# One output-projection burst per head pair, later batch-0 masks and unread matmuls in a fused attention and gated MLP kernel

## Chip, cores, metric

The kernel runs on one core of a Trainium2 chip. The metric is device microseconds of the whole program. The profile adds one execution with every instruction; its span is about 2 us below the program's time.

## The reference, cut to what matters

```python
# attention: B=8 batches, H=8 heads, S=576 queries, 16 extra "beacon" keys, D=64
k_all = concat([beacon_k, k]); v_all = concat([beacon_v, v])
scores = q @ k_all.T / sqrt(64)          # causal over the 576 keys, beacons always visible
a = softmax(scores)
x = (a @ v_all), heads side by side      # 4608 tokens x 512
# gated MLP, d_ff = 1536
out = (gelu(x @ w_gate) * (x @ w_val)) @ w_out
```

Inputs and output are float32; the kernel computes matmuls in bfloat16.

## The kernel before

One batch is 576 tokens: eight heads as four *pairs*, two heads side by side on the 128 partitions. Per pair the kernel computes transposed scores in four chunks (a, b, c, d), exponentials on ScalarE, a causal mask on the diagonal blocks, the attention product together with a product with ones (which gives the softmax denominator), and the division. The gate and value matmuls of a 512-token chunk follow after each batch, and the output projection of the chunk before (48 matmuls of 512 columns) is spread through the next batch's attention, so that TensorE has something to do while ScalarE computes exponentials. A run of such output matmuls without a break is called an *output burst* here. Batches 1 to 7 repeat the same order of work and are called *steady*; their *distance* is the time from the first output burst of one to that of the next. All engines keep program order.

```python
psum_s: 2 buffers of 2 banks   # scores, gate/value products, "wide" attention products
psum_x: 1 buffer               # attention product x_ps (x and denominator), some transposes
psum_o: 1 buffer               # output projection

def scores(b, m, c):           # chunk c of pair m: matmuls, exponential, mask
    s_ps = psum_s.tile(...)
    for t, s_lo, w, col in CHUNKS[c]:
        for hi in range(2):    # two heads on two 64-row halves of the array
            mm(s_ps[:, hi, col:col+w], qkT[r, m, 1, ...], qkT[r, m, 0, ...], True, True)
    act(expT[:, :, o:o+w], s_ps[:, :, 0:w], ACT.Exp, scale=QK_SCALE)
    # ... then for each diagonal block of the chunk:
    #   b == 0: nc.vector.tensor_tensor(min with tri);  b > 0: nc.gpsimd.affine_select

def normalize(b, m, by_act=False):
    x_sb, rec_sb = npool.tile(...), npool.tile(...)
    if by_act:                 # 1/z = exp(-ln z) on ScalarE
        act(ln_sb, z_ps, ACT.Ln)
        nc.vector.tensor_copy(x_sb, x_ps)
        act(rec_sb, ln_sb, ACT.Exp, scale=-1.0)
    else:                      # VectorE: transpose, reciprocal of one column per block, transpose back
        if m == NPAIR - 1: nc.vector.transpose(zT_sb, z_ps)      # "z first" for the last pair
        act(x_sb, x_ps, ACT.Copy)
        if m < NPAIR - 1:  nc.vector.transpose(zT_sb, z_ps)
        nc.vector.reciprocal(r_sb, ...); nc.vector.transpose(rec_sb, ...)
    nc.vector.tensor_tensor(out=xT_sb[:, m, ...], in0=x_sb, in1=rec_sb, op=ALU.mult)

# ab(m) = scores chunks a, b; cd(m) = chunks c, d; av(m) = attention product and normalize;
# o(n) = the next n output-projection matmuls of the chunk before
if b == 0:
    ab(0); transpose_pe(0,1); cd(0); ab(1); transpose_pe(0,2); cd(1); ab(2); transpose_pe(0,3)
    cd(2); ab(3); av(0); cd(3); av(1, by_act=True); av(2, wide=True); av(3, by_act=True)
else:
    o(6); ab(0); o(8); cd(0); o(6); ab(1); o(4); av(0); cd(1); o(3); ab(2); av(1)
    o(3); cd(2); o(4); ab(3); o(2); av(2); cd(3); o(5); av(3); o(7)
# then 12 x gate_val (8 matmuls, Gelu, multiply); the first leaves the two that need pair 3 to its end
# [cut: loads, DMA transposes of q and k from batch 2 on, the last stage]
```

The softmax here doesn't subtract the row's maximum and nothing guards it: scores larger than these inputs give would overflow.

Of the kernel before, what the change touches and what calls it, by code (L numbers as in the profile page):

```python
# [7 lines left out]
P = 128  # L8
B, H, S, NB, D = 8, 8, 576, 16, 64
SK = S + NB  # L10
N_TOK = B * S
D_MODEL = 512
# [40 lines left out]
def kernel(  # L53
# [59 lines left out]
    def load_qk6(b, h0, h1):  # L113
        if b not in qk6:
            qk6[b] = (
                hpool.tile([P, 2, H, 6 * D], BF16, name="qk6", tag="hT_sb"),
                npool.tile([NB, H, D], BF16, name="kb", tag="kb"),
            )
        for w, src in enumerate((q, k)):
            dma(  # L120
                qk6[b][0][0:96, w, h0:h1, :],
                src[b, h0:h1, :, :].rearrange("h (p r) d -> p h (r d)", r=6),
            )
# [30 lines left out]
    def mm(out_ap, lhsT, rhs, start, stop, **kw):  # L154
        keep(nc.tensor.matmul(out_ap, lhsT, rhs, start=start, stop=stop, **kw))  # L155

    def act(out_ap, in_ap, func, **kw):
        keep(nc.scalar.activation(out_ap, in_ap, func, **kw))  # L158


    def transpose_pe(b, m, pool, tag):
        t_ps = pool.tile([P, 3 if tag == "x" else 2, 1024], BF16, name="t_ps", tag=tag)
        qk, kb = qk6[b]

        def tr(out_ap, in_ap):
            n = in_ap.shape[0]
            keep(nc.tensor.transpose(out_ap, in_ap, ident[0:n, 0:n]))  # L167

        for w in range(2):
            for r in range(6):  # L170
                for hi in range(2):
                    tr(
                        t_ps[64 * hi : 64 * hi + 64, w, r * 96 : (r + 1) * 96],
                        qk[0:96, w, 2 * m + hi, r * D : (r + 1) * D],
                    )
        tr(t_ps[:, 1, S:SK], kb[:, 2 * m : 2 * m + 2, :])
        keep(
            nc.vector.tensor_copy(  # L178
                qkT[:, m, :, NB:SK].rearrange("p w (t r) -> p w t r", r=6),
                t_ps[:, 0:2, 0:S].rearrange("p w (r t) -> p w t r", r=6),  # L180
            )
        )
        keep(nc.vector.tensor_copy(qkT[:, m, 1, 0:NB], t_ps[:, 1, S:SK]))  # L183

    def transpose_dma(b):
        q_sb, k_sb = q_ring[b % NRING], k_ring[b % NRING]
        for j in range(5):
            for w, src, n, c in ((0, q_sb, P if j < 4 else 64, NB), (1, k_sb, P if j < 4 else 80, 0)):
                keep(
                    nc.sync.dma_start_transpose(  # L190
                        out=qkT[:, :, w, c + j * P : c + j * P + n],
                        in_=src[0:n, j, :, :].rearrange("p h d -> p (h d)"),
                    )
                )
# [3 lines left out]
    def scores(b, m, c):  # L198
        i = b * NPAIR + m
        if c == 0:  # L200
            exp_of[i] = epool.tile([P, 2, EXP_W], BF16, name="expT", tag="expT")
        expT = exp_of[i]
        s_ps = psum_s.tile([P, 2, 512], FP32, name="s_ps", tag="s")
        for t, s_lo, w, col in CHUNKS[c]:
            for hi in range(2):
                r = slice(64 * hi, 64 * hi + 64)
                mm(
                    s_ps[:, hi, col : col + w],
                    qkT[r, m, 1, t * P : (t + 1) * P],
                    qkT[r, m, 0, NB + s_lo : NB + s_lo + w],  # L210
                    True,
                    True,
                )
        o, w = CHUNK_OFF[c], CHUNK_W[c]
        act(expT[:, :, o : o + w], s_ps[:, :, 0:w], ACT.Exp, scale=QK_SCALE)
        for t, s_lo, _, _ in CHUNKS[c]:
            if s_lo != S_LO[t]:
                continue
            n = DIAG[t]
            d = expT[0 : KROWS[t], :, EXP_OFF[t] : EXP_OFF[t] + n]  # L220
            if b == 0:
                w = tri[0 : KROWS[t], NB : NB + n] if t == 0 else tri[0 : KROWS[t], 0:n]
                w = w.rearrange("p (o n) -> p o n", o=1).to_broadcast([KROWS[t], 2, n])
                keep(nc.vector.tensor_tensor(out=d, in0=d, in1=w, op=ALU.min))
            else:
                keep(
                    nc.gpsimd.affine_select(  # L227
                        out=d,
                        in_=d,
                        pattern=[[0, 2], [1, n]],  # L230
                        compare_op=ALU.is_ge,
                        fill=0.0,
                        base=NB if t == 0 else 0,
                        channel_multiplier=-1,
                    )
                )
# [32 lines left out]



    def normalize(b, m, by_act=False):
        i = b * NPAIR + m
        (x_ps, xc, _), (z_ps, zc, _) = x_of.pop(i)
        x_ps, z_ps = x_ps[:, xc : xc + S], z_ps[:, zc : zc + S]
        del exp_of[i]
        x_sb = npool.tile([P, S], FP32, name="x_sb", tag="x_sb")
        rec_sb = npool.tile([P, S], FP32, name="rec_sb", tag="rec_sb")
        if by_act:
            ln_sb = npool.tile([P, S], FP32, name="ln_sb", tag="zT_sb")  # L280
            act(ln_sb, z_ps, ACT.Ln)
            keep(nc.vector.tensor_copy(x_sb, x_ps))  # L282
            act(rec_sb, ln_sb, ACT.Exp, scale=-1.0)
        else:
            zT_sb = npool.tile([P, S], FP32, name="zT_sb", tag="zT_sb")
            r_sb = npool.tile([P, S // 32, 1], FP32, name="r_sb", tag="r_sb")

            def z_first():
                keep(nc.vector.transpose(zT_sb, z_ps))  # L289

            if m == NPAIR - 1:
                z_first()
            act(x_sb, x_ps, ACT.Copy)
            if m < NPAIR - 1:
                z_first()
            keep(nc.vector.reciprocal(r_sb, zT_sb.rearrange("p (c o) -> p c o", o=32)[:, :, 0:1]))
            keep(
                nc.vector.transpose(  # L298
                    rec_sb.rearrange("p (c o) -> p c o", o=32), r_sb.to_broadcast([P, S // 32, 32])
                )  # L300
            )
        keep(
            nc.vector.tensor_tensor(  # L303
                out=xT_sb[:, m, b * S : (b + 1) * S], in0=x_sb, in1=rec_sb, op=ALU.mult
            )
        )
# [60 lines left out]
    load_qk6(0, 0, 2)  # L367
    by_diagonal(ident, ALU.not_equal, 1.0)
    load_kb(0)
    load_qk6(0, 2, H)  # L370
    by_diagonal(tri, ALU.is_ge, 0.0)
    load_v(0)
    for i in range(3):
# [6 lines left out]
    for b in range(B):  # L380
        u = [0]

        def o(n):
            if b:
                out_mms(b - 1, u[0], u[0] + n, lambda ti: ti == 0)
                u[0] += n

        def ab(m):
            scores(b, m, 0)
            scores(b, m, 1)  # L390

        def cd(m):
            scores(b, m, 2)
            scores(b, m, 3)

        def av(m, wide=False, by_act=False):
            for t in AV_ORDER:
                attend(b, m, t, wide)
            normalize(b, m, by_act)

        keep(nc.scalar.preload_act_table_set(SET_EXP))
        if b == 0:
            ab(0)
            transpose_pe(0, 1, psum_x, "x")
            cd(0)
            ab(1)
            transpose_pe(0, 2, psum_x, "x")
            cd(1)
            ab(2)
            transpose_pe(0, 3, psum_x, "x")  # L410
            cd(2)
            ab(3)
            av(0)
            cd(3)
            av(1, by_act=True)
            av(2, wide=True)
            av(3, by_act=True)
        else:
            o(6)
            ab(0)  # L420
            o(8)
            cd(0)
            o(6)
            ab(1)
            o(4)
            av(0)
            cd(1)
            o(3)
            ab(2)
            av(1)  # L430
            o(3)
            cd(2)
            o(4)
            ab(3)
            o(2)
            av(2)
            cd(3)
            o(5)
            av(3)
            o(7)  # L440
        keep(nc.scalar.preload_act_table_set(SET_GELU))
        for fi in range(F_TILES):
            gate_val(b, fi, kk_late=fi == 0)
            if b == 0 and 6 <= fi < 10:
                transpose_pe(1, fi - 6, psum_x, "x")
            if fi == 0:
                if b + 2 < B:
                    load_qk(b + 2)
                    load_v(b + 2)
                if NPERM <= b + 1 < B:  # L450
                    transpose_dma(b + 1)
# [34 lines left out]
```

## Time and profile before

| | before |
|---|---|
| time, median of the first 3 runs | 411.73 us |
| TensorE busy | 385.3 of 408.4 us |
| start of one steady batch to the next | 43.29 us |
| first output burst (end of batch 0's work) | 60.07 us |

The page of the kernel before. Its first row of numbers is busy time per engine; the strings are 40 equal slices of the span, one digit each (tenths busy; for PEclk tenths of the granted clock); the last line gives shares of the chain of waits that ended last.

```profile
span 408.4 us, 7414 instructions
...
PE 385.3 (94%) x3036; PEld 183.0 (45%) x3036; DVE 194.7 (48%) x308; ACT 209.2 (51%) x286; POOL 156.3 (38%) x275
...
PE   2678999999999999999999999999999999999996
...
PEclk9999999999999999999999999999999999999999
...
PE 88%; ACT 4%; DVE 4%; DMA 2%; issue 1%; POOL 1%; POOLq 0%; DVEq 0%
```

TensorE is the bound almost everywhere, and the first four slices (41 us) and the last one are the only ones that are visibly thin. The Trainium skill (Trainium Kernel Development and Optimization, Performance Expectations) warns that matmul busy time is a bad measure of the distance to the best, because matmuls are pipelined.

So I read starts of single matmuls, not busy time. While nothing disturbs, 512-column matmuls start every 0.216 us. Two kinds of loss stand out in a steady batch.

The first is a wait. The TensorE timeline of the kernel before, around pair 2's first scores (columns: start, duration, engine, line, operation, operands, shape, count, and in brackets the idle time before and what ended it):

```profile
112.06 0.46 PE L155 MATMUL s_ps<-qkT 64*128 64x464 bf16 x4
112.45 0.82 PE L155 MATMUL o_ps<-wo_sb,hT_sb 128*128 128x512 bf16 x3
113.71 0.79 PE L155 MATMUL s_ps<-qkT 64*128 64x512 bf16 x8 [0.43 <-ACT expT L158]
```

And ScalarE's timeline of the kernel before at the same moment:

```profile
112.17 0.65 ACT L158 ACTIVATE x_sb<-x_ps 128x576 f32<-128x576 f32 x1 [0.79 <-PE x_ps L155]
112.72 3.36 ACT L158 ACTIVATE expT<-s_ps 128x928 bf16<-128x928 f32 x4
```

Pair 1's chunks c and d were multiplied from 112.06 on, but ScalarE copies x_sb first (0.65 us) and only then starts their exponentials. Three output matmuls are too little cover; pair 2's scores need a PSUM buffer that the exponential of c still reads. The page counts 0.43 us idle. Start to start the loss is 0.50 us, and another 0.19 us sits *inside* the eight "busy" score matmuls (0.79 us, elsewhere 0.60), since their second half waits for chunk d. All such losses in one steady batch sum to 1.33 us.

The second is the change of matmul shape. Where a full 128x128 matmul follows 64-row scores or a 64-column attention product, or the other way round, the next start comes about 0.095 us (0.092 to 0.102) later than the columns explain. The Trainium skill (TensorEngine Tiling (Array Packing), Key Properties) states that changing the tiling mode drains TensorE; it has no figure. There are 21 such changes in a batch.

Batch 0 is different: a chain of latencies. The TensorE timeline of the kernel before, from the last scores of pair 1 to pair 2's:

```profile
16.42 0.78 PE L155 MATMUL s_ps<-qkT 64*128 64x464 bf16 x4
18.66 1.01 PE L155 MATMUL s_ps<-qkT 64*128 64x512 bf16 x8 [1.46 <-DVE qkT L183]
```

After pair 1's last scores there is 1.46 us of nothing: pair 2's transposes are just being copied out of PSUM by VectorE (1.35 us), and masks stand in front of that copy. The eight score matmuls take 1.01 us here and 0.60 in a steady batch, because the array clock is still at half rate. The page's PEclk row does not show this: it is full from the first slice. The clock record in the trace (a list of grants that no view prints) begins only at 27.3 us, with full clock. The spacing of matmuls agrees: two 64-column attention matmuls take 67 ns to the next start at 26.6 us and about 30 ns in a steady batch.

### The profile page before, as it was taken

What the parts mean: (1) busy time and instruction counts of PE and PEld (TensorE: products, weight loads), DVE (VectorE), ACT (ScalarE), POOL (GpSimd) and SP (SyncE); (2) the same over time, 40 slices, a digit from 0 to 9 for tenths busy, and PEclk for the clock granted to TensorE, in tenths of its full rate; (3) what the DMA queues carried; (4) which work ended last, traced back from release to release, by engine and by line L of the source; (5) the groups of instructions that cost most, each with busy time, mean ns of one, the idle gap of its engine ahead of it and who ended that gap; (6) DMA issues with size and microseconds to landing.
All of it is one profiled execution on the core that took longest, in us unless ns stands there. A gap on an engine that the chain in (4) does not pass through costs nothing.

```text
span 408.4 us, 7414 instructions
## 1 busy us (share of the span) xinstructions
PE 385.3 (94%) x3036; PEld 183.0 (45%) x3036; DVE 194.7 (48%) x308; ACT 209.2 (51%) x286; POOL 156.3 (38%) x275
## 2 busy tenths in 40 slices
PE   2678999999999999999999999999999999999996
PEld 1344444544444444544444445444444444444442
DVE  2456463654266426633484436532664266333332
ACT  2665328643784368535763486437833684322210
POOL 8633573591239414860469035912400141000000
PEclk9999999999999999999999999999999999999999
DMA  8999991099019960999159910993023001000012
GB/s 112 186 206 205 166 126 52 29 154 165 33 48 113 148 86 27 100 164 88 53 54 173 120 53 28 153 143 73 32 67 79 27 27 53 0 0 28 26 51 104
DMA packets 139122, 36.24 MB, mean 89 GB/s; under 512 B 126800, under 2 KB 134480, under 8 KB 139088
## 3 DMA queue, kind: packets, MB, share of 16 engines
q0 software_dynamic: 103952, 19.14, 60.7%
q1 hardware_dynamic: 35136, 16.62, 18.6%
q8 instruction: 24, 0.39, 0.4%
q14 instruction: 10, 0.08, 0.1%
HBM read 38.27 MB, written 9.44 MB: 117 GB/s over the span
## 4 chain that ended last, share of the span: by engine, by line
PE 88%; ACT 4%; DVE 4%; DMA 2%; issue 1%; POOL 1%; POOLq 0%; DVEq 0%
PE gv_ps L155 45%; PE o_ps L155 23%; PE x_ps L155 12%; PE s_ps L155 7%; ACT expT L158 3%; DMA qk_103<-in_k_dram 2%; ACT x_sb L158 1%; DVE qkT L178 1%; PE t_ps L167 1%; DVE xT_sb L303 1%; POOL qk_103 L109 0%; DVE zT_sb L289 0%; DVE x_sb L282 0%; DVE hT_sb L331 0%; ACT ge_sb L158 0%
## 5 line engine op out<-in xcount | busy, mean ns | idle before, releaser
L158 ACT ACTIVATE ge_sb<-gv_ps 128x512 bf16<-128x512 f32 x108 | 64.5, 597 | 131.9 <-PE gv_ps L155 131.9
L331 DVE TENSOR_TENSOR hT_sb<-gv_ps,ge_sb 128x512 bf16<-128x512 f32 x108 | 74.7, 692 | 116.0 <-ACT ge_sb L158 116.0
L158 ACT ACTIVATE expT<-s_ps 128x1024 bf16<-128x1024 f32 (+3 forms) x128 | 103.5, 861 | 22.0 <-PE s_ps L155 20.2
L155 PE MATMUL gv_ps<-xT_sb,wg_sb 128*128 128x512 bf16 x432 | 112.3, 379 | 2.1 <-DVE xT_sb L303 1.9
L227 POOL TENSOR_SCALAR_AFFINE_SELECT expT<-expT 128x256 bf16<-128x256 bf16 (+2 forms) x140 | 53.4, 392 | 157.7 <-ACT expT L158 157.6
L155 PE MATMUL gv_ps<-xT_sb,wv_sb 128*128 128x512 bf16 x432 | 112.2, 379 | 0.0
L155 PE MATMUL o_ps<-wo_sb,hT_sb 128*128 128x512 bf16 x432 | 107.3, 381 | 0.0
L155 PEld LDWEIGHTS <-wv_sb 128*128 128x128 bf16 x432 | 42.2, 98 | 54.6 <-issue 4.6
L155 PEld LDWEIGHTS <-wg_sb 128*128 128x128 bf16 x432 | 41.8, 98 | 50.0
L155 PEld LDWEIGHTS <-hT_sb 128*128 128x128 bf16 x432 | 37.1, 98 | 47.3 <-issue 9.4
L155 PE MATMUL s_ps<-qkT 64*128 64x80 bf16 (+5 forms) x384 | 39.7, 298 | 8.6 <-DVE qkT L183 4.5
L355 DVE COPY o_sb<-o_ps 128x512 f32<-128x512 f32 x36 | 24.8, 689 | 42.5 <-PE o_ps L155 42.5
L155 PE MATMUL x_ps<-expT,ones 128*64 128x432 bf16 (+1 forms) x558 | 42.1, 247 | 0.0
L289 DVE STREAM_TRANSPOSE zT_sb<-x_ps 128x576 f32<-128x576 f32 x29 | 22.7, 781 | 32.4 <-ACT x_sb L158 32.4
L158 ACT ACTIVATE x_sb<-x_ps 128x576 f32<-128x576 f32 x29 | 18.9, 651 | 27.4 <-DVE zT_sb L289 15.8
L155 PEld LDWEIGHTS <-qkT 64*128 64x128 bf16 x384 | 13.8, 96 | 37.2 <-issue 27.3
L303 DVE TENSOR_TENSOR xT_sb<-x_sb,rec_sb 128x576 bf16<-128x576 f32 x32 | 25.1, 784 | 1.8
L155 PEld LDWEIGHTS <-ones 128*64 128x64 bf16 (+1 forms) x578 | 23.6, 112 | 4.8 <-issue 0.2
L298 DVE STREAM_TRANSPOSE rec_sb<-r_sb 128x576 f32<-128x576 f32 x30 | 23.3, 778 | 1.0
L155 PE MATMUL x_ps<-expT,v_sb_95 128*64 128x80 bf16 (+5 forms) x270 | 22.4, 253 | 1.1 <-DVE zT_sb L289 1.0
L155 PE MATMUL x_ps<-expT,v_sb_98 128*64 128x80 bf16 (+5 forms) x288 | 22.8, 246 | 0.1
L109 POOL DMA_DIRECT2D v_sb_98<-in_v_dram x20 | 17.0, 891 | 11.0 <-DMA wv_sb<-in_moe_w_val_dram 3.7
(48 smaller groups left out, 183.8 us busy)
## 6 DMA issues: line engine op xcount, KB each, us to landing
out_dram<-o_sb SPq DMA_DIRECT2D x36, 256.0 KB, 2.0
v_sb_95<-in_v_dram POOLq DMA_DIRECT2D x12, 128.0 KB, 7.7
wg_sb<-in_moe_w_gate_dram POOLq DMA_DIRECT2D x3, 512.0 KB, 11.4
wv_sb<-in_moe_w_val_dram POOLq DMA_DIRECT2D x3, 512.0 KB, 13.2
wo_sb<-in_moe_w_out_dram POOLq DMA_DIRECT2D x1, 1536.0 KB, 23.4
v_sb_98<-in_v_dram POOLq DMA_DIRECT2D x12, 128.0 KB, 10.3
q_sb_93<-in_q_dram POOLq DMA_DIRECT2D x12, 128.0 KB, 4.4
q_sb_96<-in_q_dram POOLq DMA_DIRECT2D x12, 128.0 KB, 4.1
```

The source lines that it names most:

```text
L109: keep(nc.gpsimd.dma_start(out=out_ap, in_=in_ap))
L155: keep(nc.tensor.matmul(out_ap, lhsT, rhs, start=start, stop=stop, **kw))
L158: keep(nc.scalar.activation(out_ap, in_ap, func, **kw))
L167: keep(nc.tensor.transpose(out_ap, in_ap, ident[0:n, 0:n]))
L178: nc.vector.tensor_copy(qkT[:, m, :, NB:SK].rearrange("p w (t r) -> p w t r", r=6), t_ps[:, 0:2, 0:S].rearrange("p w (r t) -> p w t r", r=6),)
L227: nc.gpsimd.affine_select(out=d, in_=d, pattern=[[0, 2], [1, n]], compare_op=ALU.is_ge, fill=0.0, base=NB if t == 0 else 0, channel_multip ...
L289: keep(nc.vector.transpose(zT_sb, z_ps))
L298: nc.vector.transpose(rec_sb.rearrange("p (c o) -> p c o", o=32), r_sb.to_broadcast([P, S // 32, 32]))
L303: nc.vector.tensor_tensor(out=xT_sb[:, m, b * S : (b + 1) * S], in0=x_sb, in1=rec_sb, op=ALU.mult)
L331: nc.vector.tensor_tensor(out=h_of[ci][:, fi, :], in0=gv_ps[:, 1, :], in1=ge_sb, op=ALU.mult)
L355: keep(nc.vector.tensor_copy(o_sb[:, ti, :], o_ps))
```

## The change

The intent: (1) in batches 1 to 7, one output burst per pair from pair 1 on instead of two, so seven bursts a batch instead of ten; (2) the last pair of each batch multiplies x straight from PSUM, which replaces "z first"; (3) in batch 0, load heads 2 and 3 before heads 4 to 7, apply masks later, and fill TensorE's idle slots with ten matmuls whose result nobody reads; (4) normalise pairs 2 and 3 of batch 0 by ScalarE and straight from PSUM.

```diff
+    def warm(b, m, n):
+        w_ps = psum_o.tile([P, D_MODEL], FP32, name="w_ps", tag="o")
+        for _ in range(n):
+            mm(w_ps, ident, qkT[:, m, 1, 0:512], True, True)
@@ scores
         act(expT[:, :, o : o + w], s_ps[:, :, 0:w], ACT.Exp, scale=QK_SCALE)
+        if b:
+            masks(b, m, c)
+
+    def masks(b, m, c):                      # the old mask code, now callable later
@@ normalize
-    def normalize(b, m, by_act=False):
+    def normalize(b, m, by_act=False, direct=False):
+        x_sb = x_ps
+        if not direct:
+            x_sb = npool.tile([P, S], FP32, name="x_sb", tag="x_sb")
         if by_act:
             act(ln_sb, z_ps, ACT.Ln)
-            keep(nc.vector.tensor_copy(x_sb, x_ps))
+            if not direct:
+                keep(nc.vector.tensor_copy(x_sb, x_ps))
         else:
-            if m == NPAIR - 1:
-                z_first()
-            act(x_sb, x_ps, ACT.Copy)
-            if m < NPAIR - 1:
-                z_first()
+            if not direct:
+                act(x_sb, x_ps, ACT.Copy)
+            keep(nc.vector.transpose(zT_sb, z_ps))
@@ loads
-    load_qk6(0, 2, H)
+    load_qk6(0, 2, 4)
+    load_qk6(0, 4, H)
@@ batch 0: [old list of calls cut]
+            for m in range(NPAIR):
+                ab(m)
+                if m == NPAIR - 1:
+                    # [masks of pair 1 (c, d) and of pair 2]
+                    av(0)
+                    # [masks of pair 3 (a, b)]
+                else:
+                    transpose_pe(0, m + 1, psum_x, "x")
+                    # [m == 2: masks of pair 0 and of pair 1 (a, b)]
+                cd(m)
+                if 1 <= m < NPAIR - 1:
+                    warm(b, m, 5)
+            # [masks of pair 3 (c, d)]
             av(1, by_act=True)
-            av(2, wide=True)
-            av(3, by_act=True)
+            av(2, wide=True, by_act=True, direct=True)
+            av(3, by_act=True, direct=True)
@@ batches 1 to 7: [old list of calls cut, it stands above]
             o(6)
             ab(0)
+            o(10)
+            cd(0)
             o(8)
+            for m in range(1, NPAIR):
+                ab(m)
+                av(m - 1)
+                cd(m)
+                o(6 if m < NPAIR - 1 else 5)
+            av(3, direct=True)
             o(7)
```

More of the change, by code (lines that the diff above doesn't have):

```diff
@@ L215, in scores @@
         act(expT[:, :, o : o + w], s_ps[:, :, 0:w], ACT.Exp, scale=QK_SCALE)
+        if b:
+            masks(b, m, c)
+    def masks(b, m, c):
+        expT = exp_of[b * NPAIR + m]
         for t, s_lo, _, _ in CHUNKS[c]:
@@ L276, in normalize @@
         del exp_of[i]
-        x_sb = npool.tile([P, S], FP32, name="x_sb", tag="x_sb")
         rec_sb = npool.tile([P, S], FP32, name="rec_sb", tag="rec_sb")
+        x_sb = x_ps
+        if not direct:
+            x_sb = npool.tile([P, S], FP32, name="x_sb", tag="x_sb")
         if by_act:
@@ L286, in normalize @@
             r_sb = npool.tile([P, S // 32, 1], FP32, name="r_sb", tag="r_sb")
-            def z_first():
-                keep(nc.vector.transpose(zT_sb, z_ps))
-            if m == NPAIR - 1:
-                z_first()
-            act(x_sb, x_ps, ACT.Copy)
-            if m < NPAIR - 1:
-                z_first()
+            if not direct:
+                act(x_sb, x_ps, ACT.Copy)
+            keep(nc.vector.transpose(zT_sb, z_ps))
             keep(nc.vector.reciprocal(r_sb, zT_sb.rearrange("p (c o) -> p c o", o=32)[:, :, 0:1]))
@@ L394, in cd, with av @@
             scores(b, m, 3)
-        def av(m, wide=False, by_act=False):
+        def av(m, wide=False, **kw):
             for t in AV_ORDER:
                 attend(b, m, t, wide)
-            normalize(b, m, by_act)
+            normalize(b, m, **kw)
         keep(nc.scalar.preload_act_table_set(SET_EXP))
         if b == 0:
-            ab(0)
-            transpose_pe(0, 1, psum_x, "x")
-            cd(0)
-            ab(1)
-            transpose_pe(0, 2, psum_x, "x")
-            cd(1)
-            ab(2)
-            transpose_pe(0, 3, psum_x, "x")
-            cd(2)
-            ab(3)
-            av(0)
-            cd(3)
+            for m in range(NPAIR):
+                ab(m)
+                if m == NPAIR - 1:
+                    for mm_ in (0, 1, 2):
+                        for c in range(4):
+                            if (mm_, c) > (1, 1):
+                                masks(0, mm_, c)
+                    av(0)
+                    for c in (0, 1):
+                        masks(0, m, c)
+                else:
+                    transpose_pe(0, m + 1, psum_x, "x")
+                    if m == 2:
+                        for mm_, c in ((0, 0), (0, 1), (0, 2), (0, 3), (1, 0), (1, 1)):
+                            masks(0, mm_, c)
+                cd(m)
+                if 1 <= m < NPAIR - 1:
+                    warm(b, m, 5)
+            for c in (2, 3):
+                masks(0, NPAIR - 1, c)
             av(1, by_act=True)
-            av(2, wide=True)
-            av(3, by_act=True)
+            av(2, wide=True, by_act=True, direct=True)
+            av(3, by_act=True, direct=True)
         else:
@@ L420 @@
             ab(0)
-            o(8)
-            cd(0)
-            o(6)
-            ab(1)
-            o(4)
-            av(0)
-            cd(1)
-            o(3)
-            ab(2)
-            av(1)
-            o(3)
-            cd(2)
-            o(4)
-            ab(3)
-            o(2)
-            av(2)
-            cd(3)
-            o(5)
-            av(3)
+            o(10)
+            cd(0)
+            o(8)
+            for m in range(1, NPAIR):
[4 more added lines that the diff above has]
+            av(3, direct=True)
             o(7)
```

## The prediction

> **What bounds the kernel now.** TensorE is busy 385.3 of 408.4 us (page, part 1), and the chain of waits is 88% TensorE. From the first gate matmul at 36.8 us on it is almost continuous: one steady batch takes 43.29 us (chain: output bursts start at 103.52 and 146.81). What can be recovered there is small. Reading starts of single matmuls in the trace of one batch (103.6 to 127.3 us), TensorE loses:
> - 1.33 us in stalls: 0.50+0.19 and 0.05+0.19 us before scores, whose PSUM buffer an exponential still reads (the ScalarE copy of x_ps, 0.65 us, stands in its way and only three output matmuls, 0.65 us, cover it); 0.10 us each before one score chunk and the last attention product; 0.20 us before the last gate matmul, waiting for xT;
> - 21 changes of matmul shape (128x128, 64-row scores, 64-column attention), each 0.095 us above the column time (512 columns otherwise start every 0.216 us).
>
> Batch 0 (0 to 36.8 us) is a latency chain: DMA landing (keys of heads 2 to 7 at 11.9 us), then 4.4 us per pair: scores, transposes, qkT copy (1.35 us, held 0.7 us by masks on VectorE), scores.
>
> **Steady batches, seven of them.** One burst per pair leaves 18 shape changes: saves 3 x 0.095 = 0.29 us. Between cd(m) and ab(m+1) now stand six output matmuls. Working a pair through with trace durations: first scores at 0; exponentials 0.49 to 2.38; attention product ends at 2.09; second score pair stalls 0.13 (for the exponential's end); x_sb copy 2.28 to 2.93; exponentials to 4.17; output burst ends 4.01, next scores start unhindered at 4.01. ScalarE needs 3.57 per pair, so TensorE stays the bound. Stalls become 3 x 0.13 plus about 0.12 for xT, 0.5 instead of 1.33. Gain about 0.8 + 0.3 = 1.1 us per batch, **7.7 us** in all. Reading PSUM directly in the last pair takes 0.65 us off ScalarE, but off the critical path.
>
> **Batch 0.** Splitting the load should land heads 2 and 3 near 8 us, so pair 1's scores start near 12.1 instead of 14.26 us. Delayed masks free the qkT copies: 0.7 us a pair. Against this stand ten matmuls. The Trainium skill (TensorE: Matmul & The Clock Gate, The HAM clock gate) says that the array runs at half rate until about 3.4 us of sustained work. The trace agrees: the same score group spans 0.73 us at 23.1 and 0.40 at 104.8; the record grants full clock at 27.3 us, after dense work from 23.1. Cold, five fillers take about 2.1 us (estimate, 512 columns at half rate), more than the freed idle (about 1.0 us), so they delay pair 2 by about 1.2 us; they pay only if the clock rises before the first attention product (2.9 cold, 1.6 us warm). VectorE then must do some 12 delayed masks (about 3.6 us) before it releases x_ps, which returns part. The tail by ScalarE (Ln, Exp) and direct multiply saves about 1 us. Gain 1.6 us if cold, 4.0 if warm near 19 us; I take **2.9 us**.
>
> **Prediction.** 411.7 - 7.7 - 2.9 = 401.1 us, range 397.5 to 405.0. Faster by over 2%: 0.77; within 2%: 0.22; slower: 0.01.
>
> **Right if** the distance between steady batches falls to about 42.2 us, the 0.5 us score stalls vanish, first gate work settles near 33 to 35 us instead of 36.8, and score groups in batch 0 run warm before 27 us.
>
> **Wrong if** ScalarE becomes the bound inside the new pair loop (waits of scores on exponentials over 0.3 us per pair), if the x_ps release through VectorE stalls attention, or if fillers stay cold and merely delay batch 0; then it lands near 404 to 406.

## The result

| | before | after |
|---|---|---|
| time, median (runs) | 411.28 us (4, 410.74 to 412.95) | 398.15 us (4, 397.49 to 398.65) |
| ratio | | 0.967 (0.964 to 0.971) |
| steady batch to steady batch | 43.29 us | 42.18 us |
| first output burst | 60.07 us | 55.25 us |
| full clock granted (trace's clock record) | 27.3 us | 18.6 us |

A ratio is the mean time of one kernel's runs over that of the other's of the same rounds, so it is not quite the ratio of the medians in the table.

The page of the changed kernel, the same lines:

```profile
span 396.2 us, 7413 instructions
...
PE 382.3 (97%) x3046; PEld 185.9 (47%) x3046; DVE 190.5 (48%) x304; ACT 202.2 (51%) x280; POOL 156.3 (39%) x277
...
PE   3889999999999999999999999999999999999996
...
PE 79%; DMA 8%; POOL 3%; DVE 3%; ACT 3%; issue 2%; SPq 2%; POOLq 0%; ACTq 0%
```

The second slice went from 6 to 8 and the third from 7 to 8: batch 0 is denser. The chain's shares moved too, with 8% on DMA. That is a trap: the chain now runs back through the DMA transposes that fill qkT and the loads before them, since in two of the six distances between batches scores wait for one. It is charged with the whole duration of each DMA (6.97 and 6.69 us for the two transposes). The wait itself is small. The waits of TensorE in the changed kernel (who waited, for whom, total us, times, longest):

```profile
PE s_ps L155 <- DMA qkT<-k_sb_94: 0.2, 1, 0.2
```

Two of the six distances are 42.41 and 42.50 instead of 42.18 us.

The distance of steady batches can be read from the chain: each begins with six output matmuls. The chain of the kernel before (start, duration, what):

```profile
103.52 1.29 PE o_ps L155 x6
...
146.81 1.29 PE o_ps L155 x6
```

The same of the changed kernel:

```profile
97.45 1.29 PE o_ps L155 x6
...
139.63 1.29 PE o_ps L155 x6
```

The TensorE timeline of the changed kernel from pair 2's chunks c and d to pair 3's scores, which answers to the wait shown above:

```profile
109.81 0.60 PE L155 MATMUL s_ps<-qkT 64*128 64x464 bf16 x4
110.34 1.47 PE L155 MATMUL o_ps<-wo_sb,hT_sb 128*128 128x512 bf16 x6
111.75 0.60 PE L155 MATMUL s_ps<-qkT 64*128 64x512 bf16 x8
```

And its ScalarE timeline, one pair earlier (the same pattern):

```profile
105.95 0.66 ACT L158 ACTIVATE x_sb<-x_ps 128x576 f32<-128x576 f32 x1
106.48 1.38 ACT L158 ACTIVATE expT<-s_ps 128x928 bf16<-128x928 f32 x2
108.21 1.89 ACT L158 ACTIVATE expT<-s_ps 128x1024 bf16<-128x1024 f32 x2 [0.35 <-PE s_ps L155]
```

The scores after the burst start without a bracket: no idle. The copy x_sb (105.95) still stands ahead of the exponentials of c and d (106.48), but six output matmuls now cover both, and the next scores find their buffer free. In return chunk d waits a little for the exponential of b: 0.60 us instead of 0.46 for the four matmuls at 109.81. Start to start, each of three pairs loses 0.14 us, and the first gate product 0.11 us for xT: 0.54 us where 1.33 were lost.

Batch 0 in the changed kernel's TensorE timeline:

```profile
14.61 2.32 PE L155 MATMUL w_ps<-qkT,ident 128*128 128x512 bf16 x5
16.86 1.01 PE L155 MATMUL s_ps<-qkT 64*128 64x512 bf16 x8
...
19.65 1.25 PE L155 MATMUL w_ps<-qkT,ident 128*128 128x512 bf16 x5
20.83 0.60 PE L155 MATMUL s_ps<-qkT 64*128 64x512 bf16 x8
```

The first five unread matmuls (w_ps) take 2.32 us, the second five 1.25, and scores fall from 1.01 to 0.60 us between pairs 2 and 3: the clock rises in between. The same 512-column matmuls start every 0.427 us in the first five and every 0.216 in the second.

### The profile page after: what moved, and what is told of

The parts are those of the page before. It is cut to its first block, busy times and chain, and to the rows that moved or that the text cites. A ratio compares the mean times of both kernels' runs of the same rounds, so it can differ in the third digit from the quotient of the medians.

```text
span 396.2 us, 7413 instructions
## 1 busy us (share of the span) xinstructions
PE 382.3 (97%) x3046; PEld 185.9 (47%) x3046; DVE 190.5 (48%) x304; ACT 202.2 (51%) x280; POOL 156.3 (39%) x277
## 4 chain that ended last, share of the span: by engine, by line
PE 79%; DMA 8%; POOL 3%; DVE 3%; ACT 3%; issue 2%; SPq 2%; POOLq 0%; ACTq 0%
PE gv_ps L155 36%; PE o_ps L155 23%; PE x_ps L155 11%; PE s_ps L155 8%; DMA qkT<-k_sb_94 3%; DMA v_sb_98<-in_beacon_v_dram 2%; SPq L196 2%; ACT expT L158 2%; DMA k_sb_97<-in_k_dram 2%; POOL k_sb_97 L109 1%; PE t_ps L167 1%; DVE qkT L178 1%; POOL q_sb_96 L109 1%; PE w_ps L155 1%; DMA kb<-in_beacon_k_dram 1%
## 5 line engine op out<-in xcount | busy, mean ns | idle before, releaser
L238 POOL TENSOR_SCALAR_AFFINE_SELECT expT<-expT 128x256 bf16<-128x256 bf16 (+2 forms) x140 | 52.4, 388 | 142.2 <-ACT expT L158 142.1
L155 PE MATMUL o_ps<-wo_sb,hT_sb 128*128 128x512 bf16 x432 | 103.6, 380 | 0.0
L155 PEld LDWEIGHTS <-hT_sb 128*128 128x128 bf16 x432 | 38.8, 98 | 46.6 <-issue 2.8
L155 PE MATMUL x_ps<-expT,ones 128*64 128x432 bf16 (+1 forms) x558 | 41.2, 243 | 0.0
L155 PEld LDWEIGHTS <-qkT 64*128 64x128 bf16 x384 | 14.8, 96 | 30.4 <-issue 21.8
L155 PE MATMUL x_ps<-expT,v_sb_95 128*64 128x80 bf16 (+5 forms) x270 | 21.5, 245 | 1.5 <-DVE zT_sb L304 1.1
L155 PE MATMUL x_ps<-expT,v_sb_98 128*64 128x80 bf16 (+5 forms) x288 | 22.8, 246 | 0.0
L109 POOL DMA_DIRECT2D v_sb_98<-in_v_dram x20 | 17.0, 868 | 11.9 <-DMA wv_sb<-in_moe_w_val_dram 3.7
L109 POOL DMA_DIRECT2D v_sb_95<-in_v_dram x20 | 17.0, 889 | 2.5 <-DMA k_sb_94<-in_k_dram 2.3
L312 DVE TENSOR_TENSOR xT_sb<-x_sb,rec_sb 128x576 bf16<-128x576 f32 x23 | 17.4, 758 | 0.9
```

Of the source, the lines that this page charges most:

```text
L109: keep(nc.gpsimd.dma_start(out=out_ap, in_=in_ap))
L155: keep(nc.tensor.matmul(out_ap, lhsT, rhs, start=start, stop=stop, **kw))
L238: nc.gpsimd.affine_select(out=d, in_=d, pattern=[[0, 2], [1, n]], compare_op=ALU.is_ge, fill=0.0, base=NB if t == 0 else 0, channel_multip ...
L312: nc.vector.tensor_tensor(out=xT_sb[:, m, b * S : (b + 1) * S], in0=x_sb, in1=rec_sb, op=ALU.mult)
```

## The experiments

All ran with five rounds, on three chips; the runs of the kernel before on those chips had medians of 411.22, 411.16 and 410.56 us. "Batch 0" is the time from the first transposes to the first output burst, in the one profiled run; it leaves out the start of the first load, which varies by some tenths.

| run | median us | ratio (95% interval) | steady distance | full clock at | batch 0 |
|---|---|---|---|---|---|
| before | 411.28 | 1 | 43.29 | 27.3 | 55.3 |
| after | 398.15 | 0.967 (0.964, 0.971) | 42.18 | 18.6 | 50.8 |
| after_again | 397.62 | 0.968 (0.965, 0.971) | 42.18 | 16.5 | 50.2 |
| bursts_only | 402.57 | 0.979 (0.978, 0.981) | 42.25 | 27.6 | 55.0 |
| batch0_only | 409.52 | 0.996 (0.993, 0.999) | 43.86 | 17.8 | 51.2 |
| batch0_direct | 405.38 | 0.987 (0.983, 0.990) | 43.22 | 17.6 | 50.3 |
| no_direct | 402.78 | 0.980 (0.977, 0.984) | 42.84 | 17.4 | 50.6 |
| one_load | 400.50 | 0.974 (0.972, 0.975) | 42.18 | 19.8 | 53.6 |
| old_tail | 399.26 | 0.971 (0.968, 0.973) | 42.18 | 17.9 | 52.0 |
| no_fill | 399.01 | 0.970 (0.968, 0.971) | 42.18 | 24.1 | 51.6 |
| fill_only | 409.80 | 0.997 (0.993, 1.000) | 43.29 | 18.6 | 53.4 |
| masks_now | 398.18 | 0.968 (0.966, 0.970) | 42.18 | 19.2 | 51.5 |
| early_fill | 397.10 | 0.965 (0.963, 0.968) | 42.18 | 13.9 | 49.8 |
| early_fill2 | 397.25 | 0.966 (0.963, 0.969) | 42.18 | 18.1 | 49.7 |

The steady distance is the most frequent of the six. No kernel with a timed result failed the comparison with the reference.

### bursts_only: the new order of bursts and nothing else

```diff
 (kernel before, batches 1 to 7)
-            o(8); cd(0); o(6); ab(1); o(4); av(0); cd(1); o(3); ab(2); av(1)
-            o(3); cd(2); o(4); ab(3); o(2); av(2); cd(3); o(5); av(3); o(7)
+            o(10); cd(0); o(8)
+            for m in range(1, NPAIR):
+                ab(m); av(m - 1); cd(m); o(6 if m < NPAIR - 1 else 5)
+            av(3); o(7)
```

> The kernel before with only the new order of batches 1 to 7 (one output burst per pair; no direct reading of PSUM, batch 0 untouched). Theory A (the six-matmul burst hides the two exponentials, and three shape changes fall away): stalls per steady batch drop from 1.33 to about 0.6 us and shape changes from 21 to 18, the distance of steady batches falls from 43.3 to about 42.2 us, and the time falls by about 7 us, to 404. Rival B (only the shape changes count, the stalls come back elsewhere because ScalarE is the bound): about 2 us, to 409.

402.57 us, and 42.25 us between batches. From the chain of bursts_only (the window cuts the last burst short):

```profile
101.88 1.29 PE o_ps L155 x6
...
144.13 1.08 PE o_ps L155 x5
```

Stalls fall to 0.61 us, shape changes to 18. Of the fall of the distance, 1.04 us, 0.72 come from stalls and 3 x 0.095 from shape changes, so rival B, shape changes alone, falls. Over seven batches this is 7.3 us; the median fell by 8.65. The rest is not the change's: batch 0 ended 0.5 us earlier, since its second load landed that much earlier, and the profiled run of the kernel before, 410.45 us, was itself 0.8 us below the median of its runs here.

### batch0_only and batch0_direct: the old order of bursts in the changed kernel

```diff
 (changed kernel, batches 1 to 7)
-            [one burst per pair] ... av(3, direct=True)
+            [the old order]      ... av(3)                  # batch0_only
+            [the old order]      ... av(3, direct=True)     # batch0_direct
```

> The changed kernel with the old order of output bursts in batches 1 to 7 (so batch 0's changes alone, plus direct reading nowhere but in batch 0). If the two parts add up: steady batches 43.3 us apart again, first output burst at about 55.4 us, time about 5 us below the kernel before, 406. If the steady part needs batch 0's part or the other way round, the sum of this gain and that of the bursts alone misses 13 us by over 2 us.

409.52 us: only 1.6 below the kernel before. With bursts_only at 8.6 this does not add up to 13.1, which at first looked as if the parts helped each other. But batches were 43.86 us apart, more than the 43.29 of the kernel before. My edit had left the last pair with neither "z first" nor the direct reading, since the change had taken away the first. The next kernel puts that right.

> Batch 0's changes with the old order of output bursts, and the last pair of each later batch reading x from PSUM. The earlier run of the old order without that reading kept neither the early VectorE transpose nor the direct reading, and its steady batches were 43.87 us apart. Theory A (that lost order alone is why the two parts did not add up): distance back to about 43.2 us, time 405.7, so that this gain (5.5) and the 8.6 of the bursts alone come to 13 to 14. Rival B (batch 0's part is worth only 1.6 us by the clock on the wall, the profile misleads): about 409.

405.38 us, distance 43.22. That is 1.3% below the kernel before; with the 2.1% of bursts_only it makes 3.4%, against 3.3 and 3.2% for both together. The parts add up, and rival B falls.

### no_direct: the last pair copied out of PSUM again

```diff
 (changed kernel, batches 1 to 7)
-            av(3, direct=True)
+            av(3)
```

> The changed kernel, but the last pair of batches 1 to 7 copies x to SBUF on ScalarE before the VectorE transpose. Theory A (the copy then lies in front of the last xT): the gate matmuls that need it wait about 0.6 instead of 0.1 us, steady batches are 42.7 instead of 42.2 us apart, time 401.5 to 402. Rival B (seven output and six gate matmuls hide it): no difference.

402.78 us against 397.62 of after_again on the same chip, and 42.84 us per batch. The timeline of no_direct at the end of a batch (TensorE, ScalarE and VectorE lines, others left out):

```profile
118.00 0.65 ACT L158 ACTIVATE x_sb<-x_ps 128x576 f32<-128x576 f32 x1 [1.36 <-issue]
...
118.69 0.78 DVE L304 STREAM_TRANSPOSE zT_sb<-x_ps 128x576 f32<-128x576 f32 x1 [0.57 <-ACT x_sb L158]
...
121.43 0.38 PE L155 MATMUL gv_ps<-xT_sb,wg_sb 128*128 128x512 bf16 x1 [0.60 <-DVE xT_sb L312]
```

The same place in the changed kernel:

```profile
117.31 0.78 DVE L304 STREAM_TRANSPOSE zT_sb<-x_ps 128x576 f32<-128x576 f32 x1
...
119.23 0.76 DVE L312 TENSOR_TENSOR xT_sb<-x_ps,rec_sb 128x576 bf16<-128x576 f32 x1
...
120.04 0.38 PE L155 MATMUL gv_ps<-xT_sb,wg_sb 128*128 128x512 bf16 x1
```

Without direct reading, the copy x_sb (0.65 us) comes first, the VectorE transpose waits for it, and the last xT comes 0.6 us too late for the gate matmul. With it the transpose starts as soon as the product is there. A multiply straight from PSUM costs no more: 0.76 us in both. So direct reading is off the critical path only when compared with "z first", to which it adds 0.07 us per batch (42.25 against 42.18 in bursts_only). With z first gone it is worth 0.66 us per batch.

### one_load: heads 2 to 7 in one piece

```diff
-    load_qk6(0, 2, 4)
-    load_qk6(0, 4, H)
+    load_qk6(0, 2, H)
```

> The changed kernel with heads 2 to 7 loaded in one piece again. Theory A (the split lets pair 1 start earlier, and all of batch 0 follows): pair 1's scores start near 14 instead of 11.6 us and the time is about 2.4 us longer, 400.5. Rival B (later pairs are held by something else, so the early start is lost in waiting): under 0.5 us.

400.50 us, 2.35 more than the changed kernel, as expected by theory A. TensorE's timeline of one_load before pair 1's scores:

```profile
10.63 0.69 PE L167 MATMUL t_ps<-ident,qk 96*64 96x96 bf16 x12 [1.38 <-DMA qk<-in_q_dram]
12.88 0.69 PE L167 MATMUL t_ps<-ident,qk 96*64 96x96 bf16 x12 [1.55 <-DMA qk<-in_k_dram]
```

The transposes wait 1.38 and 1.55 us for q and k, and pair 1's scores start at 15.23 instead of 11.61 us, later than the 14 expected, because the load landed later than in the kernel before (12.88 against 11.91 us). In the four profiled runs with one piece that landing varied from 11.2 to 12.9 us, so the trace shows the order of events and the median the size. This load is the largest single part of batch 0's gain.

### old_tail: batch 0's last pairs normalised as before

```diff
-            av(2, wide=True, by_act=True, direct=True)
-            av(3, by_act=True, direct=True)
+            av(2, wide=True)
+            av(3, by_act=True)
```

> The changed kernel with pairs 2 and 3 of batch 0 normalised as before (VectorE transposes for pair 2, x copied out of PSUM for both). Theory A (VectorE is the last engine of batch 0, and the direct multiply takes about three of its 0.75 us operations off the end): the last xT is about 1.3 us later than 31.9 us, time 399.4. Rival B (ScalarE's chain of logarithm and exponential sets the end either way): no difference over 0.3 us.

399.26 us, 1.1 more. VectorE's timeline of old_tail at the end of batch 0's attention:

```profile
31.65 0.75 DVE L297 COPY x_sb<-x_ps 128x576 f32<-128x576 f32 x1
32.51 0.76 DVE L312 TENSOR_TENSOR xT_sb<-x_sb,rec_sb 128x576 bf16<-128x576 f32 x1
```

The changed kernel at the same place:

```profile
29.13 0.76 DVE L312 TENSOR_TENSOR xT_sb<-xs_ps,rec_sb 128x576 bf16<-128x576 f32 x1 [0.24 <-ACT rec_sb L158]
31.14 0.76 DVE L312 TENSOR_TENSOR xT_sb<-x_ps,rec_sb 128x576 bf16<-128x576 f32 x1 [1.25 <-ACT rec_sb L158]
```

In old_tail VectorE still copies x before the last multiply, without idling, and ends at 33.27 us; in the changed kernel only multiplies are left, it waits for ScalarE, and ends at 31.90. The first transposes began 0.14 us apart, so about 1.2 us is the tail's. The intervals of the two ratios still overlap. But from pair 1's scores to the first output burst old_tail takes 44.8 us, and the five profiled runs with the changed kernel's batch 0 (after, after_again, batch0_only, batch0_direct, no_direct) take 43.0 to 43.9. Theory A holds.

### no_fill and fill_only: the unread matmuls

```diff
 (no_fill: changed kernel)               (fill_only: kernel before, batch 0)
-        warm(b, m, 5)                   +        cd(1); warm(b, 1, 5); ab(2)
                                         +        cd(2); warm(b, 2, 5); ab(3)
```

> The changed kernel without the ten unread matmuls. Theory A (they release the TensorE clock early, which pays more than they cost): pair 2 starts its scores about 1.3 us earlier (15.5 instead of 16.9), but the clock is granted only some 5 us later than 18.6, the first attention product runs cold (2.9 instead of 1.6 us), and the time is about 1 us longer, 399. Rival B (the clock would rise as early without them, and they are mere cost): about 1.3 us shorter, 396.8.

> The kernel before with nothing but the ten unread matmuls in batch 0. Theory A (their worth is the clock): they are longer than the 1.5 us idle slots while cold, so pair 2 starts about 0.7 us later than 18.7, but the clock is granted before the first attention product; the time falls by 0.5 to 1 us. Rival B (mere cost): 0.7 to 1.4 us longer.

Without them pairs 2 and 3 do start earlier, pair 2 by half of what was expected, and everything after is slower. TensorE's timeline of no_fill from pair 3's scores:

```profile
20.00 1.01 PE L155 MATMUL s_ps<-qkT 64*128 64x512 bf16 x8 [0.83 <-ACT expT L158]
20.94 0.69 PE L155 MATMUL x_ps<-expT,v_sb 128*64 128x496 bf16 x4
```

The changed kernel at the same place, behind the scores shown above (20.83):

```profile
21.36 0.44 PE L155 MATMUL x_ps<-expT,v_sb_95 128*64 128x496 bf16 x4
```

Pair 2's scores start at 16.23 (16.86 with fillers), pair 3's at 20.00 (20.83), but the clock comes only at 24.1 us, and the attention product's matmuls of 496 columns take 0.69 us instead of 0.44. The second product starts at 25.48 instead of 24.56.

The price in time is smaller than the scatter. no_fill is 0.9 us above the changed kernel by medians, but the intervals overlap, and batch 0 took 51.6 us where five profiled runs with the same batch 0 as the changed kernel took 50.2 to 51.2. In fill_only the ten matmuls take 1.4 us off the kernel before, with an interval that just leaves out 1. Pair 1 to pair 2 grew from 4.40 to 5.10 us, as expected by theory A, and the clock came at 18.6 instead of 27.3 us. The landing of loads can be left out by counting from pair 1's scores to the first output burst: fill_only takes 44.5 us against 45.8 of the kernel before, no_fill 44.4 against 43.0 to 43.9 of the five. All point the same way, so rival B, mere cost, has nothing for it; the size is around 1 us and not known better.

The scatter has a reading. The Trainium skill (TensorE: Matmul & The Clock Gate, The HAM clock gate) says that the activity window of about 3.4 us is free-running and does not start with the kernel. The five runs with the same batch 0 fit this: full clock came anywhere between 16.5 and 18.6 us, a spread of less than one window. The window's length shows too: in all 14 traces the grant of full clock lasts a whole number of 3.413 us (111 of them, 378.88 us, in the changed kernel; 109, 372.05 us, in no_fill). No run controls the phase, so that it is the cause of the scatter is not shown.

### masks_now: masks right behind the exponentials

```diff
-        if b:
-            masks(b, m, c)
+        masks(b, m, c)
 (and the later calls for batch 0 taken out)
```

> The changed kernel with batch 0's masks right behind each exponential, as before. Theory A (masks hold up the qkT copies by about 0.7 us per pair, but for pairs 2 and 3 the filler matmuls hide most of that, and the masks then no longer hold the x_sb copy of pair 1 for 0.4 us): 0.6 us longer, 398.8. Rival B (the masks are the main gain of batch 0): 2 us longer, 400.

398.18 us: no difference to 398.15, where 0.6 was expected. In the trace, pair 1's scores start 0.86 us later and waits of scores on the qkT copies grow from 1.5 to 3.3 us in total, so masks do hold the copies; but the second attention product is 1.16 us later and the last xT only 0.81, of which 0.13 is a later first load. Whether the delayed masks are worth nothing or the 0.6 us is open: this run's interval is 1.6 us wide. They are not the main gain of batch 0, so rival B falls.

### after_again, early_fill, early_fill2: can the clock come earlier?

```diff
+    junk = const.tile([P, 512], BF16, name="junk", tag="junk")     # memset to 1.0
+    def early(n): n matmuls of junk into an unread psum_o tile
+    early(6)                                  # while the first load is on its way
     transpose_pe(0, 0, psum_s, "s")
+    early(3)
@@ batch 0
-                if 1 <= m < NPAIR - 1:
-                    warm(b, m, 5)
+                if m == 0:
+                    early(2)                  # early_fill2: 1
+                elif m < NPAIR - 1:
+                    warm(b, m, 5)             # early_fill2: 3 (m == 1), 2 (m == 2)
```

> The changed kernel with eleven more unread matmuls: six before the first transposes, while the first load is on its way, three before pair 0's scores, two before pair 1's. Theory A (the clock is what limits batch 0 until it is released, and work that waits for no data can release it): the clock is granted between 5 and 12 us instead of at 18.6, pair 3's scores start about 2 us earlier than 20.8, and the time is up to 2 us shorter, 396.5. Rival B (transposes break the busy window, or the ScalarE exponentials bound batch 0): within 0.5 us of 398.15.

> The early fillers with fewer later ones (one before pair 1, three before pair 2, two before pair 3), since with the clock granted near 14 us the later ones held up pair 3's scores by 0.95 us. If they were only in the way: pair 3's scores near 19.4 us and the time 0.4 to 0.6 us below the first early version, 396.5. If the clock falls back or rises late without them, 398 or more, and the runs scatter by over 2 us.

> The changed kernel unaltered, as the reference for the other three on this chip: 398.2 us, within 0.5, if chips agree.

The first gave 397.10 us, with runs from 395.79 to 398.10; the clock came at 13.9 us, later than the 5 to 12 of theory A, and pair 3's scores at 19.96, 0.9 us earlier where 2 were expected. The second gave 397.25; its clock came at 18.1 us in the profiled run, no earlier than in the changed kernel, and pair 3's scores at 19.91 where 19.4 was expected. The unaltered kernel on the second version's chip gave 397.62, 0.6 us below the 398.2 expected. Both versions are a little lower than the changed kernel, and no interval separates them from it. This is inconclusive: the matmuls during the load may be worth half a microsecond, and did not release the clock reliably; why, no run tests. Exponentials follow each other with gaps of 0.62 us between pairs in early_fill, so ScalarE is close to being batch 0's bound there.

## Why the prediction was right, and where it was off

**Steady batches: right in mechanism and size.** 42.2 us was forecast, 42.18 came; stalls of 0.13 us per pair were worked out from trace durations, 0.14 came; 0.12 for the last gate product, 0.11 came. From the first output burst to the last gate stage, 7.4 us were gained, where 7.7 were forecast; the missing part is the new waits for DMA transposes (the two longer distances, 0.55 us together), while batch 1 gained a little more than the others (1.25 us). bursts_only shows that this part stands alone.

**Batch 0: right in direction, under-sized.** The term was 2.9 us; the first output burst came 4.8 us earlier, 0.3 of it from an earlier landing of the first load, so 4.5 like for like. The step that was mis-sized is "Gain 1.6 us if cold, 4.0 if warm near 19 us; I take 2.9". The clock was full by 18.6 us, and in all five profiled runs with this batch 0, so the warm figure was the right one. No run isolates the 0.5 us that are left. A candidate is VectorE: "some 12 delayed masks (about 3.6 us)", which were to return part of the gain, were fifteen in 2.90 us. They ended at 23.24 us, and VectorE then still waited 0.48 us for the copy x_sb before it could release x_ps, so they returned nothing there. Of the parts, one_load and old_tail show 2.35 and 1.1 us; the fillers are worth around 1 us, with the scatter named above; for masks nothing could be shown.

**The direct reading: "off the critical path" was true only by comparison with "z first".** no_direct shows 5 us for the changed kernel without it.

**The total** of 401.1 was 3 us too long: 1.9 us come from batch 0 as the profile shows it, less 0.3 from the steady part. The profiles' spans differ by 12.2 us and the medians by 13.1, since the profiled run of the kernel before was 0.8 us faster than the median of its four runs; and that median is itself 0.45 us below the 411.73 from which the forecast started. The result, 398.15, lies near the lower end of the stated range (397.5).

**Signs named beforehand.** The 0.5 us stalls vanished; score groups of batch 0 were warm before 27 us; gate work settled at 31.95 us, better than the 33 to 35 forecast. None of the three dangers came: ScalarE did not become the bound, VectorE's release of x_ps stalled attention by 1.1 us (1.0 before) and by a new 0.4 us, both small, and the fillers did not stay cold.

## What to carry to other kernels

When an engine is nearly full, sum the delays between starts of its instructions over one period, name each one's releaser, and work one period of the new order through with durations from the trace; here that gave the new period to 0.02 us (42.2 worked out, 42.18 measured). In this kernel interleaved filler work did best in pieces as long as the dependency that it covers, one piece per round: short pieces left stalls, and each change of matmul shape cost time. When an ablation does not add up, look at the period before inventing an interaction: taking one part back may have removed what another part had replaced.

## What the Trainium skill lacked or had wrong

- TensorEngine Tiling (Array Packing), Key Properties: it says that a change of mode drains TensorE, without a figure. Here each change between 128x128, 64-row and 64-column matmuls cost about 0.095 us at full clock.
- TensorE: Matmul & The Clock Gate, The HAM clock gate and Why this matters for your kernels: it tells to keep TensorE busy, but not what share of the window suffices, and it names warm-up matmuls for benchmarks only. Here unread matmuls inside a kernel did the same: ten of them moved the grant from 24.1 us to between 16.5 and 18.6 in kernels with an otherwise equal batch 0. Eleven more, early ones gave 13.9 in one version; ten early ones with fewer later ones gave 18.1 in another.
- The same page: it warns that clock records can be unreliable. Here the records of 27.3 and 18.6 us agreed with the spacing of matmuls, but the profile page's row of granted clock showed full clock from the start, before the first record.
- VectorE: DVE Perf Modes, Rules for kernel authors: for work on a matmul's output it offers to accept the 1x mode or, where many operations follow, to copy PSUM to SBUF first. It makes no exception for a float32 operation on two tensors, which the page's own perf-mode tier table puts at 1x from either memory. The runs agree with the table: this multiply of 128x576 takes 0.76 us from PSUM and 0.76 us from SBUF, so there was nothing to accept.
